# Attention and expert kernel: each unit in four stages a turn apart, state decay and kp on GpSimd, routing in four batches

## The chip, the cores and the metric

One core of one Trainium2 chip. The metric is device time in microseconds (us), from the first to the last instruction of the core. The engines are PE (TensorE matmuls; PEld its weight loads), DVE (VectorE), ACT (ScalarE), POOL (GpSimd) and SP (SyncE, whose queue issues most DMA transfers).

A run is called slow, and left out of the ratios, when it is over 1.5% above the fastest run of its kernel in the set; the others are called fast. Between sets on different chips the same kernel differed by up to 3%: the medians of the kernel before in the sets below are 473 to 488 us. So every comparison is made with runs of the kernel before on the same chip in the same set.

## The reference

A linear attention with a complex, data-dependent decay, then a mixture of experts that sends each row to its best expert. Batch 4, heads 8, sequence 768, head dimension 48; 8 experts of width 1024.

```python
mag = np.sqrt(a_re * a_re + a_im * a_im)
scale = np.minimum(mag, 0.999) / (mag + 1e-06)
a_re_n, a_im_n = a_re * scale, a_im * scale
for t in range(S):                                  # state S_re + i S_im, D x D for each head
    new_re = ar * S_re - ai * S_im
    new_im = ar * S_im + ai * S_re
    S_re, S_im = new_re + outer(k[t], v[t]), new_im
    y[t] = q[t] @ S_re
# rows of y -> logits by w_gate -> one expert for each row
out[row] = gate * relu(x[row] @ w1[e]) @ w2[e]
```

## The kernel before

The sequence is cut into 6 chunks of 128 steps, which with the 4 batches gives 24 units (g, b). Two units make a group: the elementwise work (logarithms, angles, exponentials) is done by group, and ScalarE loads its function tables twice for each. A unit then takes cumulative moduli and angles, and makes the scaled `Qh`, `KW` (whose first part is k scaled by `kp`), `V`:

```python
def hats(x, i):
    ...
    nc.vector.tensor_tensor(P[:], cs[:, i], both(pm[:, 0, i]), Alu.mult)        # 768 elements a partition
    nc.vector.tensor_tensor(kp[:], qk[:, 1, i], pm[:, 1, i], Alu.mult)          # 384
    ...
    nc.vector.tensor_tensor(Qh[:], P[:], both(qk[:, 0, i]), Alu.mult)
    nc.vector.tensor_tensor(KW[:, :, 0:C]..., cs[:, i], both(kp[:]), Alu.mult)
```

`front` transposes both on PE, copies them out on ScalarE and makes the masked product W at once; `back` makes Y and the new state, and the rows from Y at once:

```python
def front(g, b):                                    # transposes -> KT, QT -> W
    ...
            nc.scalar.copy(T[name][:, h4:h4 + 4], tp)
    ...
        nc.vector.tensor_tensor(KW[:, h4:h4 + 4, C:], wp, mask..., Alu.mult)

def back(g, b, KW, V, cB, QT):                      # Zs, Y and U, state, rows
    ...
            nc.scalar.copy(yT[:, js], py[:, :, C:])
    ...
        nc.vector.tensor_tensor(t1[:], U[:], cB[:, :, 0:1, :]..., Alu.mult)     # 384
        nc.vector.tensor_tensor(t2[:], U[:], cB[:, :, 1:2, :]..., Alu.mult)     # 384
        nc.vector.tensor_tensor(new[:, :, 0], t1[:, :, 0], t2[:, :, 1], Alu.add)       # 192
        nc.vector.tensor_tensor(new[:, :, 1], t1[:, :, 1], t2[:, :, 0], Alu.subtract)  # 192
    ...
        nc.tensor.matmul(xw[:, j, :], yT[:, j, :], sel[:, j, :], start=True, stop=True)
```

The text of the kernel gives the instructions and their dependencies. The order in which each engine issues them is chosen when the program is built, by a scheduler that places whatever it reckons to be ready first. The engines then keep to that order: in the trace of the changed kernel the loop's operations on VectorE (260), ScalarE (340) and GpSimd (140) all start in the built order.

Of the kernel before, what the change touches and what calls it, by code (L numbers as in the profile page):

```python
# [23 lines left out]
def gate_loop(nc, ctx, tc, cpool, ident, q, k, v, a_re, a_im, sel, lg, x_rows, casts, make_router):  # L24
# [120 lines left out]
    def moduli(x):  # L145
        cs, lm = box.pop(("cs", x))
        pm = el.tile([L, 2, NG, H, D], F32, name="pm")
# [10 lines left out]
    def hats(x, i):  # L158
# [7 lines left out]
        nc.vector.tensor_tensor(kp[:], qk[:, 1, i], pm[:, 1, i], Alu.mult)  # L166
# [3 lines left out]
        KW = un.tile([L, H, C + L], F32, name="KW", bufs=4)  # L170
        nc.vector.tensor_tensor(KW[:, :, 0:C].rearrange("t h (c d) -> t h c d", c=2), cs[:, i], both(kp[:]), Alu.mult)
        V = un.tile([L, H, 64], F32, name="V", bufs=4)
# [3 lines left out]
        if g < G - 1:  # L176
            cB = un.tile([128, J, 2, D], F32, name="cB", bufs=4)
            for u in range(2):
                nc.sync.dma_start(out=cB[u * 64:(u + 1) * 64].rearrange("p j c d -> p j (c d)"), in_=c_scr[g * B + b].rearrange("(j u c) -> u j c", u=2, c=C)[u][None].broadcast_to([64, J, C]))
        box["unit", g, b] = Qh, KW, V, cB  # L180

    def front(g, b):
        Qh, KW, V, cB = box.pop(("unit", g, b))
        T = {}
        for name, src in (("KT", KW[:, :, 0:C]), ("QT", Qh.rearrange("t h c d -> t h (c d)"))):
            T[name] = un.tile([C, H, L], F32, name=name)
            for h4 in range(0, H, 4):
# [3 lines left out]
                nc.scalar.copy(T[name][:, h4:h4 + 4], tp)  # L191
        for h4 in range(0, H, 4):
            wp = bank([L, 4, L], "wp")
            for i in range(4):
                for u in range(2):
                    nc.tensor.matmul(wp[u * 64:(u + 1) * 64, i, :], T["KT"][:, h4 + i, u * 64:(u + 1) * 64], T["QT"][:, h4 + i, :], start=True, stop=True)  # L196
            nc.vector.tensor_tensor(KW[:, h4:h4 + 4, C:], wp, mask[:, None, :].broadcast_to([L, 4, L]), Alu.mult)  # L197
        return KW, V, cB, T["QT"]
# [3 lines left out]
    def back(g, b, KW, V, cB, QT):  # L202
# [27 lines left out]
        if more:  # L230
            t1 = un.tile([128, J, 2, D], F32, name="t1", bufs=1)
            t2 = un.tile([128, J, 2, D], F32, name="t2", bufs=1)
            new = un.tile([128, J, 2, D], F32, name=f"state{b}", bufs=2)
            nc.vector.tensor_tensor(t1[:], U[:], cB[:, :, 0:1, :].broadcast_to([128, J, 2, D]), Alu.mult)
            nc.vector.tensor_tensor(t2[:], U[:], cB[:, :, 1:2, :].broadcast_to([128, J, 2, D]), Alu.mult)
            nc.vector.tensor_tensor(new[:, :, 0], t1[:, :, 0], t2[:, :, 1], Alu.add)
            nc.vector.tensor_tensor(new[:, :, 1], t1[:, :, 1], t2[:, :, 0], Alu.subtract)
            state[b] = new

        xw = bank([L, J, sel.shape[2]], "xw")  # L240
# [8 lines left out]
    NX = len(groups)  # L249
    EXP, TRIG = "natural_log_exp_and_others", "trig_and_small"  # L250
    table(EXP)
# [4 lines left out]
    table(TRIG)  # L256
    angles(0)
    rt = make_router(ctx, ps, bank)
    table(EXP)
    moduli(0)  # L260
    logs(1)
    load_a(2)
    for i in range(NG):
        hats(0, i)
    load_qk(1)
    table(TRIG)
    angles(1)
    made = front(*groups[0][0])
    open_ = []
    late = []  # L270
    w = 0
    for x in range(NX):
        for i, (g, b) in enumerate(groups[x]):
            w += 1
            ahead = front(*order[w]) if w < len(order) and i + 1 < NG else None
            if i == 0:

                table(EXP)
                if x + 1 < NX:
                    moduli(x + 1)  # L280
                for f in late:
                    f(act)
                late = []
                if x + 2 < NX:
                    logs(x + 2)
                    load_qk(x + 2)
                if x + 3 < NX:
                    load_a(x + 3)
            back(g, b, *made)
            if x + 1 < NX:  # L290
                hats(x + 1, i)
            if i == NG - 1:
                if x + 2 < NX:
                    table(TRIG)
                    angles(x + 2)
# [408 lines left out]
```

## Time and profile before

| | us |
|---|---|
| median of the runs, before | 473.3 (472.5 to 478.4) |
| profiled run | 476.2, clock 0.914 (a run marked slow) |
| last matmul of the rows ends | 343.7 |
| experts after it | 132.5 |
| a group in the loop, 158 to 315 us | 26.1 |

The loop over the units is the part that the change touches. The lines of the profile that carry this are in the prediction.

### The profile page before, as it was taken

What the parts mean: (1) busy time and instruction counts of PE and PEld (TensorE: products, weight loads), DVE (VectorE), ACT (ScalarE), POOL (GpSimd) and SP (SyncE); (2) the same over time, 40 slices, a digit from 0 to 9 for tenths busy, and PEclk for the clock granted to TensorE, in tenths of its full rate; (3) what the DMA queues carried; (4) which work ended last, traced back from release to release, by engine and by line L of the source; (5) the groups of instructions that cost most, each with busy time, mean ns of one, the idle gap of its engine ahead of it and who ended that gap; (6) DMA issues with size and microseconds to landing.
All of it is one profiled execution on the core that took longest, in us unless ns stands there. A gap on an engine that the chain in (4) does not pass through costs nothing.

```text
span 476.2 us, 8571 instructions
## 1 busy us (share of the span) xinstructions
PE 355.6 (75%) x3141; PEld 267.6 (56%) x3141; DVE 294.5 (62%) x673; ACT 259.6 (55%) x442; POOL 110.2 (23%) x138
## 2 busy tenths in 40 slices
PE   0518887678749698877978696989824998899874
PEld 0206564556636476655757484768613766667552
DVE  2683876869478887978797887765261433344321
ACT  3575767567736757776686758675312222223221
POOL 6401030200202002110202000000013566566512
PEclk9957889799979989998999899899955999999988
DMA  9979299987968899997999550100038799899991
GB/s 153 148 135 130 61 185 156 175 125 129 169 119 155 130 182 170 181 166 130 164 164 193 93 109 18 35 1 18 10 126 331 263 357 353 300 347 315 351 379 65
DMA packets 166844, 80.84 MB, mean 170 GB/s; under 512 B 145431, under 2 KB 157196, under 8 KB 166802
## 3 DMA queue, kind: packets, MB, share of 16 engines
q1 hardware_dynamic: 151810, 59.92, 53.3%
q0 software_dynamic: 14992, 20.37, 21.8%
q8 instruction: 25, 0.41, 0.4%
q14 instruction: 17, 0.14, 0.1%
HBM read 85.68 MB, written 21.12 MB: 224 GB/s over the span
## 4 chain that ended last, share of the span: by engine, by line
PE 32%; ACT 20%; issue 16%; DVE 15%; DMA 8%; POOL 6%; SPq 2%; POOLq 0%; DVEq 0%; ACTq 0%
PE wp L196 7%; PE py L218 5%; ACT sq L82 5%; PE xw L242 5%; ACT KT L191 4%; DMA xg<-x_rows,idx 3%; PE u L136 3%; POOL xg L573 3%; POOL out_dram L615 3%; DMA ab<-in_a_im_dram 3%; DVE s L111 2%; PE py L221 2%; DVE Qh L169 2%; ACT L79 2%; PE tKT L190 2%
## 5 line engine op out<-in xcount | busy, mean ns | idle before, releaser
L218 PE MATMUL py<-KW,V 128*64 128x224 f32 x384 | 63.6, 390 | 0.0
L196 PE MATMUL wp<-QT,KT 96*64 96x128 f32 x768 | 48.7, 281 | 14.6 <-ACT QT L191 14.1
L197 DVE TENSOR_TENSOR KW<-wp,mask 128x512 f32<-128x512 f32 x48 | 32.9, 688 | 37.6 <-PE wp L196 37.4
L196 PEld LDWEIGHTS wp<-QT,KT 96*64 96x64 f32 x768 | 42.5, 139 | 20.8 <-ACT QT L191 20.8
L242 PE MATMUL xw<-sel,yT 128*128 128x104 f32 x192 | 34.4, 309 | 25.7 <-ACT yT L229 25.6
L596 PE MATMUL h_ps<-xgT,w1t 128*128 128x256 bf16 (+1 forms) x456 | 47.7, 266 | 4.3 <-DMA w1t<-w1b 4.3
L242 PEld LDWEIGHTS xw<-sel,yT 128*128 128x128 f32 x192 | 27.9, 206 | 38.8 <-ACT yT L229 31.8
L136 PE MATMUL u<-tan,turn 128*128 128x384 f32 x48 | 25.3, 615 | 31.7 <-ACT tan L82 31.7
L221 PE MATMUL py<-QT,Zs 96*48 96x128 f32 x320 | 37.7, 283 | 13.4 <-ACT Zs L208 13.3
L596 PEld LDWEIGHTS <-w1t 128*128 128x128 bf16 x456 | 40.1, 103 | 11.5 <-DMA w1t<-w1b 5.5
L600 ACT ACTIVATE hT<-h_ps 128x512 bf16<-128x512 f32 x31 | 18.5, 597 | 50.2 <-PE h_ps L596 44.3
L607 PE MATMUL y_ps<-w2t,hT 128*128 128x384 bf16 x248 | 43.7, 327 | 2.3 <-DMA w2t<-w2b 2.3
L573 POOL DMA_INDIRECT xg<-x_rows,idx x31 | 30.1, 972 | 60.5 <-ACT idx L559 51.3
L191 ACT COPY KT<-tKT 96x512 f32<-96x512 f32 x48 | 25.8, 581 | 32.7 <-PE tKT L190 32.6
L615 POOL DMA_INDIRECT out_dram<-y_sb,idx x31 | 31.4, 1013 | 47.0 <-ACT y_sb L611 42.7
L598 DVE TENSOR_SCALAR hT<-h_ps 128x512 bf16<-128x512 f32 x31 | 21.4, 692 | 29.2 <-PE h_ps L596 28.1
L218 PEld LDWEIGHTS py<-KW,V 128*64 128x64 f32 x384 | 32.9, 148 | 10.4 <-issue 4.7
L115 POOL TENSOR_SCALAR neg<-ab 128x768 bf16<-128x768 f32 x12 | 25.7, 2143 | 54.5 <-DMA ab<-in_a_re_dram 32.2
L221 PEld LDWEIGHTS py<-QT,Zs 96*48 96x48 f32 x320 | 25.0, 128 | 22.4 <-ACT Zs L208 17.6
L173 POOL MEMSET V<- 128x128 f32 x24 | 4.7, 203 | 135.3 <-PE py L218 89.4
L79 ACT ACT_TABLE_LOAD x27 | 34.6, 1283 | 1.3 <-PEq L688 0.8
L607 PEld LDWEIGHTS <-hT 128*128 128x128 bf16 x248 | 23.5, 98 | 17.0 <-issue 1.5
(135 smaller groups left out, 700.4 us busy)
## 6 DMA issues: line engine op xcount, KB each, us to landing
w1t<-w1b SPq DMA_DIRECT2D x19, 768.0 KB
w2t<-w2b SPq DMA_DIRECT2D x19, 768.0 KB
w1b<-in_moe_w_dram POOLq DMA_DIRECT2D x8, 768.0 KB, 7.9
w2b<-in_moe_w_dram POOLq DMA_DIRECT2D x8, 768.0 KB, 9.3
ab<-in_a_re_dram SPq DMA_DIRECT2D x24, 192.0 KB
ab<-in_a_im_dram SPq DMA_DIRECT2D x24, 192.0 KB
qk<-in_q_dram SPq DMA_DIRECT2D x24, 192.0 KB
qk<-in_k_dram SPq DMA_DIRECT2D x24, 192.0 KB
```

The lines of the kernel that those rows point to most:

```text
L79: then(nc.scalar.preload_act_table_set(name))
L136: nc.tensor.matmul(u, turn[:], tan[:, i], start=True, stop=False)
L191: nc.scalar.copy(T[name][:, h4:h4 + 4], tp)
L196: nc.tensor.matmul(wp[u * 64:(u + 1) * 64, i, :], T["KT"][:, h4 + i, u * 64:(u + 1) * 64], T["QT"][:, h4 + i, :], start=True, stop=True)
L197: nc.vector.tensor_tensor(KW[:, h4:h4 + 4, C:], wp, mask[:, None, :].broadcast_to([L, 4, L]), Alu.mult)
L218: nc.tensor.matmul(py[u * 64:(u + 1) * 64, i, :], V[:, 2 * j + u, :], KW[:, 2 * j + u, :], start=True, stop=(g == 0))
L221: nc.tensor.matmul(py[u * 64:u * 64 + D, i, C:], Zs[:, j, u * 64:u * 64 + D], QT[:, 2 * j + u, :], start=False, stop=True)
L242: nc.tensor.matmul(xw[:, j, :], yT[:, j, :], sel[:, j, :], start=True, stop=True)
L573: nc.gpsimd.indirect_dma_start(out=xg[:], out_offset=None, in_=x_rows, in_offset=bass.IndirectOffsetOnAxis(ap=idx[:, s, 0:1], axis=0))
L596: nc.tensor.matmul(h_ps[:, f, :], w1t[:, k, ff * 128:(ff + 1) * 128], xgT[:, k, :], start=(k == 0), stop=(k == KD - 1))
L607: nc.tensor.matmul(y_ps[:], hT[:, f, s * 128:(s + 1) * 128], w2t[:, f, :], start=(f == 0), stop=(f == NF - 1))
L615: sc = nc.gpsimd.indirect_dma_start(out=out, out_offset=bass.IndirectOffsetOnAxis(ap=idx[:, s, 1:2], axis=0), in_=y_sb[:], in_offset=None, ...
```

## The change

The intent: spread a unit over more turns, so that no engine waits for what another has just begun (W finds its transposes, the rows find Y, both made a turn earlier); relieve VectorE by moving `kp` and the state decay to GpSimd, which is mostly idle; and fewer, larger routing batches. Buffers are shifted to make room. The core of the diff:

```diff
-        nc.vector.tensor_tensor(kp[:], qk[:, 1, i], pm[:, 1, i], Alu.mult)
+        nc.gpsimd.tensor_tensor(kp[:], qk[:, 1, i], pm[:, 1, i], Alu.mult)
 ...
-    def front(g, b):
+    def values(g, b):      # V, cB                 (buffers 4 -> 3)
+    def turned(g, b):      # transposes, KT, QT
+    def inner(g, b):       # W
 ...
-    def back(g, b, KW, V, cB, QT):
+    def outer(g, b):       # Zs, Y, U, state
 ...
-            nc.vector.tensor_tensor(t1[:], U[:], cB..., Alu.mult)
-            nc.vector.tensor_tensor(t2[:], U[:], cB..., Alu.mult)
-            nc.vector.tensor_tensor(new[:, :, 0], t1[:, :, 0], t2[:, :, 1], Alu.add)
-            nc.vector.tensor_tensor(new[:, :, 1], t1[:, :, 1], t2[:, :, 0], Alu.subtract)
+            nc.gpsimd.tensor_tensor(t1[:], U[:], cB..., Alu.mult)
+            nc.gpsimd.tensor_tensor(t2[:], U[:], cB..., Alu.mult)
+            nc.gpsimd.tensor_tensor(new[:, :, 0], t1[:, :, 0], t2[:, :, 1], Alu.add)
+            nc.gpsimd.tensor_tensor(new[:, :, 1], t1[:, :, 1], t2[:, :, 0], Alu.subtract)
+    def rows(g, b):        # rows, logits
 ...
+    takes = {7: 0, 15: 8, 19: 16, 23: 20}          # routing batches of 8, 8, 4 and 4 tiles, not six of 4
+    for w in range(NU + 1):
+        unit(values, w + 1)
+        unit(turned, w + 2)
+        unit(inner, w + 1)
+        unit(outer, w)
+        unit(rows, w - 1)
+        if w % NG == 0:
+            exps(w // NG + 2)
+        hat(w + 3)
+        if w % NG == NG - 1:
+            trigs(w // NG + 3)
```

More of the change, by code (lines that the diff above doesn't have):

```diff
@@ L146, in moduli @@
         cs, lm = box.pop(("cs", x))
-        pm = el.tile([L, 2, NG, H, D], F32, name="pm")
+        pm = el.tile([L, 2, NG, H, D], F32, name="pm", bufs=1)
         for i in range(NG):
@@ L169, in hats @@
         nc.vector.tensor_tensor(Qh[:], P[:], both(qk[:, 0, i]), Alu.mult)
-        KW = un.tile([L, H, C + L], F32, name="KW", bufs=4)
+        KW = un.tile([L, H, C + L], F32, name="KW", bufs=5)
         nc.vector.tensor_tensor(KW[:, :, 0:C].rearrange("t h (c d) -> t h c d", c=2), cs[:, i], both(kp[:]), Alu.mult)
-        V = un.tile([L, H, 64], F32, name="V", bufs=4)
+        box["hats", g, b] = Qh, KW
+    def values(g, b):
+        V = un.tile([L, H, 64], F32, name="V", bufs=3)
         nc.gpsimd.memset(V[:, :, D:64], 0.0)
@@ L176, in hats @@
         if g < G - 1:
-            cB = un.tile([128, J, 2, D], F32, name="cB", bufs=4)
+            cB = un.tile([128, J, 2, D], F32, name="cB", bufs=3)
             for u in range(2):
                 nc.sync.dma_start(out=cB[u * 64:(u + 1) * 64].rearrange("p j c d -> p j (c d)"), in_=c_scr[g * B + b].rearrange("(j u c) -> u j c", u=2, c=C)[u][None].broadcast_to([64, J, C]))
-        box["unit", g, b] = Qh, KW, V, cB
-    def front(g, b):
-        Qh, KW, V, cB = box.pop(("unit", g, b))
+        box["values", g, b] = V, cB
+    def turned(g, b):
+        Qh, KW = box.pop(("hats", g, b))
         T = {}
-        for name, src in (("KT", KW[:, :, 0:C]), ("QT", Qh.rearrange("t h c d -> t h (c d)"))):
-            T[name] = un.tile([C, H, L], F32, name=name)
+        for name, src, bufs in (("KT", KW[:, :, 0:C], 2), ("QT", Qh.rearrange("t h c d -> t h (c d)"), 3)):
+            T[name] = un.tile([C, H, L], F32, name=name, bufs=bufs)
             for h4 in range(0, H, 4):
@@ L191, in front @@
                 nc.scalar.copy(T[name][:, h4:h4 + 4], tp)
+        box["turned", g, b] = KW, T["KT"], T["QT"]
+    def inner(g, b):
+        KW, KT, QT = box.pop(("turned", g, b))
         for h4 in range(0, H, 4):
@@ L195, in front @@
                 for u in range(2):
-                    nc.tensor.matmul(wp[u * 64:(u + 1) * 64, i, :], T["KT"][:, h4 + i, u * 64:(u + 1) * 64], T["QT"][:, h4 + i, :], start=True, stop=True)
+                    nc.tensor.matmul(wp[u * 64:(u + 1) * 64, i, :], KT[:, h4 + i, u * 64:(u + 1) * 64], QT[:, h4 + i, :], start=True, stop=True)
             nc.vector.tensor_tensor(KW[:, h4:h4 + 4, C:], wp, mask[:, None, :].broadcast_to([L, 4, L]), Alu.mult)
-        return KW, V, cB, T["QT"]
+        box["inner", g, b] = KW, QT
     state = {}
-    def back(g, b, KW, V, cB, QT):
+    def outer(g, b):
+        KW, QT = box.pop(("inner", g, b))
+        V, cB = box.pop(("values", g, b))
         if g:
@@ L232, in back @@
             t2 = un.tile([128, J, 2, D], F32, name="t2", bufs=1)
-            new = un.tile([128, J, 2, D], F32, name=f"state{b}", bufs=2)
-            nc.vector.tensor_tensor(t1[:], U[:], cB[:, :, 0:1, :].broadcast_to([128, J, 2, D]), Alu.mult)
-            nc.vector.tensor_tensor(t2[:], U[:], cB[:, :, 1:2, :].broadcast_to([128, J, 2, D]), Alu.mult)
-            nc.vector.tensor_tensor(new[:, :, 0], t1[:, :, 0], t2[:, :, 1], Alu.add)
-            nc.vector.tensor_tensor(new[:, :, 1], t1[:, :, 1], t2[:, :, 0], Alu.subtract)
+            new = un.tile([128, J, 2, D], F32, name=f"state{b}", bufs=1)
+            nc.gpsimd.tensor_tensor(t1[:], U[:], cB[:, :, 0:1, :].broadcast_to([128, J, 2, D]), Alu.mult)
+            nc.gpsimd.tensor_tensor(t2[:], U[:], cB[:, :, 1:2, :].broadcast_to([128, J, 2, D]), Alu.mult)
+            nc.gpsimd.tensor_tensor(new[:, :, 0], t1[:, :, 0], t2[:, :, 1], Alu.add)
+            nc.gpsimd.tensor_tensor(new[:, :, 1], t1[:, :, 1], t2[:, :, 0], Alu.subtract)
             state[b] = new
+        box["outer", g, b] = yT
+    def rows(g, b):
+        yT = box.pop(("outer", g, b))
         xw = bank([L, J, sel.shape[2]], "xw")
@@ L249, in gate_loop, with exps, trigs, unit @@
     NX = len(groups)
+    NU = len(order)
     EXP, TRIG = "natural_log_exp_and_others", "trig_and_small"
+    open_ = []
+    late = []
+    takes = {7: 0, 15: 8, 19: 16, 23: 20}
+    def exps(x):
+        if x < NX + 1:
+            table(EXP)
+        if x < NX:
+            moduli(x)
+        for f in late:
+            f(act)
+        late.clear()
+        if x + 1 < NX:
+            logs(x + 1)
+            load_qk(x + 1)
+        if x + 2 < NX:
+            load_a(x + 2)
+    def trigs(x):
+        if x < NX:
+            table(TRIG)
+            angles(x)
+    def unit(stage, w):
+        if 0 <= w < NU:
+            stage(*order[w])
+    def hat(w):
+        if w < NU:
+            hats(w // NG, w % NG)
     table(EXP)
@@ L255, in gate_loop @@
     load_qk(0)
-    table(TRIG)
-    angles(0)
-    rt = make_router(ctx, ps, bank)
-    table(EXP)
-    moduli(0)
-    logs(1)
-    load_a(2)
-    for i in range(NG):
-        hats(0, i)
-    load_qk(1)
-    table(TRIG)
-    angles(1)
-    made = front(*groups[0][0])
-    open_ = []
-    late = []
-    w = 0
-    for x in range(NX):
-        for i, (g, b) in enumerate(groups[x]):
-            w += 1
-            ahead = front(*order[w]) if w < len(order) and i + 1 < NG else None
-            if i == 0:
-                table(EXP)
-                if x + 1 < NX:
-                    moduli(x + 1)
-                for f in late:
-                    f(act)
-                late = []
-                if x + 2 < NX:
-                    logs(x + 2)
-                    load_qk(x + 2)
-                if x + 3 < NX:
-                    load_a(x + 3)
-            back(g, b, *made)
-            if x + 1 < NX:
-                hats(x + 1, i)
-            if i == NG - 1:
-                if x + 2 < NX:
-                    table(TRIG)
-                    angles(x + 2)
-                if w < len(order):
-                    ahead = front(*order[w])
-            made = ahead
-            for _ in range(1):
-                if casts:
-                    cast = casts.pop(0)()
-                    tc.add_manual_dep(cast.ins, chain[-1].ins.name, mybir.DependencyInfo(mybir.DependencyClass.Sync, mybir.DependencyReason.DATA), reason="spreads the casts over the turns")
-            open_ = [t for t in open_ if next(t, True) is None]
-            if b == B - 1:
-                open_.append(rt.take(g * B, (g + 1) * B, late))
-                next(open_[-1])
@@ L307, in gate_loop @@
-    table(EXP)
+    trigs(0)
+    exps(0)
+    hat(0)
+    hat(1)
+    unit(turned, 0)
+    trigs(1)
+    rt = make_router(ctx, ps, bank)
+    exps(1)
+    hat(2)
+    unit(inner, 0)
+    unit(turned, 1)
+    trigs(2)
+    unit(values, 0)
+    for w in range(NU + 1):
[9 more added lines that the diff above has]
+            trigs(w // NG + 3)
+        if casts:
+            cast = casts.pop(0)()
+            tc.add_manual_dep(cast.ins, chain[-1].ins.name, mybir.DependencyInfo(mybir.DependencyClass.Sync, mybir.DependencyReason.DATA), reason="spreads the casts over the turns")
+        open_ = [t for t in open_ if next(t, True) is None]
+        if w - 1 in takes:
+            open_.append(rt.take(takes[w - 1], w, late))
+            next(open_[-1])
@@ L346, in __init__ @@
         rc = self.rc = ctx.enter_context(tc.tile_pool(name="rc", bufs=1))
-        self.rp = ctx.enter_context(tc.tile_pool(name="rp", bufs=3))
+        self.rp = ctx.enter_context(tc.tile_pool(name="rp", bufs=2))
         self.tile_of = [b * G + g for g in range(G) for b in range(B)]
@@ L395, in take @@
         last = m1 == len(self.tile_of)
-        M = 4
+        M = 8
         def t(name, shape, dt=F32):
@@ L420, in take @@
             so_far.append(self.acc)
-            acc = rp.tile([TP, E], BF16, name="acc", bufs=16)
+            acc = rp.tile([TP, E], BF16, name="acc", bufs=20)
             if self.acc is None:
@@ L462, in take @@
         for i in range(n):
-            lo = rp.tile([TP, 2, 128], BF16, name="lo", bufs=4)
+            lo = rp.tile([TP, 2, 128], BF16, name="lo", bufs=8)
             nc.vector.tensor_scalar(lo[:, 0], self.iob[:, 0:128], part[:, 0, i:i + 1], self.p1[:], Alu.is_equal, Alu.mult)
             nc.vector.tensor_scalar(lo[:, 1], self.iob[:, 0:128], part[:, 0, i:i + 1], float(TP * self.tile_of[m0 + i]), Alu.is_equal, Alu.mult)
-            hi = rp.tile([TP, self.NC], BF16, name="hi", bufs=4)
+            hi = rp.tile([TP, self.NC], BF16, name="hi", bufs=8)
             nc.vector.tensor_scalar(hi[:], self.iob[:, 0:self.NC], part[:, 1, i:i + 1], None, Alu.is_equal)
```

## The prediction

> **What bounds the kernel now.** I read the page's busy line and slices first, to see where each engine and the DMA are full.
>
> ```profile
> PE 355.6 (75%) x3141; PEld 267.6 (56%) x3141; DVE 294.5 (62%) x673; ACT 259.6 (55%) x442; POOL 110.2 (23%) x138
> ...
> PE   0518887678749698877978696989824998899874
> ...
> DVE  2683876869478887978797887765261433344321
> ACT  3575767567736757776686758675312222223221
> POOL 6401030200202002110202000000013566566512
> ...
> DMA  9979299987968899997999550100038799899991
> ```
>
> A slice is 11.9 us. Slices 0 to 3 are the start-up, 4 to 28 the attention loop, the rest the experts. In the loop no engine is full; the DMA row is nearly full up to slice 21, and almost empty after. The change touches only the first 344 us.
>
> Then the busy time of each engine by stretch (columns: stretch, length, PE, PEld, DVE, ACT, POOL busy, clock, DMA share, GB/s):
>
> ```profile
> 158.00:210.00 52.00, 42.36 (x414) 33.22 (x410) 43.39 (x102) 37.32 (x62) 8.21 (x10) 0.97 0.99 165
> 210.00:262.00 52.00, 42.37 (x409) 32.90 (x406) 43.15 (x103) 37.07 (x61) 8.22 (x10) 0.97 0.93 162
> 262.00:315.00 53.00, 43.50 (x405) 33.78 (x405) 41.02 (x100) 37.07 (x61) 0.82 (x4) 0.94 0.30 57
> ```
>
> Each stretch is two groups of two units. Per group: DVE 21.6 us, PE 21.2, ACT 18.6, DMA 24.2 to 25.7. Now the chain of waits, for the pace: the modulus matmul (ls) opens each group.
>
> ```profile
> 124.50 8.56 DMA ab<-in_a_im_dram
> ...
> 158.47 0.86 PE ls L150 x2
> ...
> 210.17 0.86 PE ls L150 x2
> ...
> 261.81 0.86 PE ls L150 x2
> ...
> 314.90 0.86 PE ls L150 x2
> ...
> 342.48 1.18 PE xw L242 x8
> ```
>
> From 158.47 to 314.90 six groups pass: 26.1 us a group, with the DMA full (two stretches) and with it at 0.30 (the third). So DMA does not set this pace; a relay between PE, ACT and DVE does, and DMA adds a stall now and then (8.56 us at 124.50). The relay shows in the page's idle column:
>
> ```profile
> L197 DVE TENSOR_TENSOR KW<-wp,mask 128x512 f32<-128x512 f32 x48 | 32.9, 688 | 37.6 <-PE wp L196 37.4
> L242 PE MATMUL xw<-sel,yT 128*128 128x104 f32 x192 | 34.4, 309 | 25.7 <-ACT yT L229 25.6
> L221 PE MATMUL py<-QT,Zs 96*48 96x128 f32 x320 | 37.7, 283 | 13.4 <-ACT Zs L208 13.3
> L196 PE MATMUL wp<-QT,KT 96*64 96x128 f32 x768 | 48.7, 281 | 14.6 <-ACT QT L191 14.1
> ```
>
> W waits for the copies of the transposes made just before it, the rows waited 25.6 us for yT made just before them, Y for Zs. These are what the stages a turn apart should remove.
>
> **What the Trainium skill says.** "GPSIMD Engine Reference", section 3.1: a tensor_tensor add of 2048 fp32 takes 4497 ns on GpSimd against 2293 ns on VectorE, about twice. The trace before has no two-input work on GpSimd; its one large op, neg (768 elements), takes 2.13 us. "SBUF — State Buffer", section "Who interferes with whom": a VectorE instruction with two SBUF inputs contends with a GpSimd instruction that reads SBUF, and the later one blocks until the first is done. The trace agrees only in part: under a neg of 2.21 us, tan took 1.57 us instead of 0.96, and a one-hot 0.60 instead of 0.19, so some 0.4 to 0.6 us lost, not the whole. "DMA: Bandwidth & Descriptors", Specifications: full rate needs transfers of at least 512 B. Here 145431 of 166844 packets are under that: the first 50 us moved 38071 packets of about 180 bytes with the DMA 90% busy, so 1.18 ns each over 16 engines, at 135 GB/s; the experts' large ones run above 300.
>
> **The change part by part.**
>
> DVE. Per group it loses two kp (0.551 us), four state products (0.552) and four state sums (0.352): 1.10 + 2.21 + 1.41 = 4.7 us. It goes from 21.6 to 16.9 us.
>
> GpSimd. It gains them. An estimate from the skill's 2.2 ns an element, with a little dispatch: 0.95 us for 384 elements, 0.55 for 192, so 6 x 0.95 + 4 x 0.55 = 7.9 us. With neg 2.1, two memsets 0.4 and two cast issues 0.71 and 0.86, about 12 us of a group: half busy, not a bound. Its reads (10 us) meet some 10 us of DVE's two-input work; at random 10 x 10 / 25 = 4 us of overlap, half of it paid by DVE: 19 us, still under the pace. The state is needed four turns later, so its slower decay is hidden; kp is behind P and Qh (1.9 us) on DVE and mostly hidden.
>
> PE. Its work is the same. The instruction order of the changed kernel is now: transposes of unit w+2, W of w+1, state transposes, half of Y of w, rows of w-1, rest of Y. W finds KT and QT, and the rows find yT, made a turn earlier. In throughput a turn is 1.8 (16 transposes) + 2.0 (W) + 0.6 + 2.8 (state and Y) + 1.25 (rows) = 8.4 us, plus 3.4 a group for u and ls: 20.2 us a group. What remains is one serial piece a group: rows, table load 1.28, tan 0.85, u 2.3, fr 1.1, cs 1.8, table 1.28, exps.
>
> ACT. 18.6 us of work a group is unchanged. Walking its new order from the end of tan: it must wait 3.3 us until u and the first transposes have passed PE; about 1 us for the second ls, behind Y; and about 1 us in small waits for U and for s. 18.6 + 5.3 = 24 us a group.
>
> DMA. The same packets. With casts, 24.2 to 25.7 us a group, and the 16 casts still sit in the first 16 turns. So those eight groups can hardly go below 25; the ninth, without casts, takes ACT's 24.
>
> Start-up. The new prologue does one more group of elementwise work before the loop. In the trace before, the table for the exps of group 1 ends at 43.7 us, 19.9 us after that of group 0 (23.8). One more such round is 63.6, and the first U and yT copies (1.5 us) give 65 for the exps of group 2; before, they come at 76.
>
> End. In the changed kernel the exps of group 11, the last, come at turn 18, with PE already some way into the turn: 2.7 us of it left, then three full turns without elementwise work at 8.7, then 6.8, 4.8 and 1.3 us as the stages run out: 41.7 us. Before, 343.7 - 315.8 = 28 us remain there.
>
> Sum: 65 + 9 x 25.0 + 41.7 = 331.7 us at the last row matmul, against 343.7 (342.48 + 1.18) before: 12 us less. Routing in four batches of 4 or 8 in place of six of 4 saves two sets of about 14 small DVE operations of 0.17 us (5 us) off the path; the last batch is still four tiles, so the 132 us after it do not move. 473.3 - 12 = **461 us**.
>
> **The rivals.**
>
> One: DMA becomes the bound. For it: 0.99 and 0.93 busy at the present pace, and the 8.56 us wait for ab. If each cast group takes 25.7 us and stalls come on top (26.4), the sum is 344: no gain, about 473. Against it: in 50 to 262 us the share is 0.91, so about 19 us are idle, and casts may fall behind into the turns after 16, where DMA is nearly free. If they do, ACT's 24 us hold throughout: 65 + 216 + 41.7 = 323, or 452 us.
>
> Two: GpSimd in order becomes a relay. neg waits for DMA (32.2 us in total before), casts wait for ACT, and kp, the V memset (so V's load, now issued only a turn ahead with three buffers instead of four) and the state stand behind them. One late ab load then delays kp, KW and the transposes. With the port lock slower than my estimate this costs 1 to 2 us a group: 27 us a group, 65 + 243 + 41.7 = 350, or 479 us.
>
> Three: DVE was the true bound, and 4.7 us less is worth nearly all of it: 26.1 - 4.7 = 21.4 us a group, 65 + 193 + 41.7 = 300, or 430. Against it: DMA cannot serve that in the cast groups, and PE needs 20.2 with a serial piece besides.
>
> **Range and chances.** The pace of a group decides: 24 gives 452, 25 gives 461, 26 gives 470; the start-up may be off by 3 us and the end by 4. Range 449 to 473. Faster by over 2% is under 463.9, that is a pace under 25.3: 0.60. Within 2% (up to 482.8): 0.33. Slower: 0.07.
>
> **What would show it.** Right: the ls marks 24 to 25 us apart, ACT the best filled engine with its idle time at the transposes' copies after tan, DMA at 0.95 or more up to about 255 us, the waits of W on QT and of the rows on yT nearly gone, DVE near 19 us and GpSimd near 12 us a group, exps of group 2 near 65 us, last rows near 332. Wrong: marks at 26 with DMA full (rival one); DVE's two-input operations clearly longer than 0.95 us, or PE waiting for transposes' inputs through kp (rival two); marks at 22 or less, which would say that DMA's busy share is not a service limit; or the last 132 us moving at all.

## The result, and the profile after

The changed kernel takes 494.3 us (493.8 to 497.3, four fast runs) against 472.9 of the kernel before in the same set. The ratio is 1.048, with a 95% interval of 1.042 to 1.054: slower by 4.8%. A ratio here is always the mean time of one kernel's fast runs over the mean of the other's fast runs of the same rounds, so it is not quite the ratio of the medians. The profiled run after is fast (492.6 us); that of before, a slow one, would make the loss look smaller than it is.

The page after, the busy line and the slices of GpSimd and the DMA engines:

```profile
PE 359.8 (73%) x3141; PEld 269.0 (55%) x3141; DVE 284.2 (58%) x539; ACT 259.2 (53%) x439; POOL 223.9 (45%) x242
...
POOL 6243063744646446454364636262004176566612
...
DMA  9949646979697797849949785112007699999992
```

The same work, and a POOL row that is now half full in the loop; but the DMA row, which was nearly full before up to slice 21, has gaps. The same stretches as in the prediction (columns: stretch, length, PE, PEld, DVE, ACT, POOL busy, clock, DMA share, GB/s):

```profile
158.00:210.00 52.00, 41.21 (x349) 30.25 (x349) 36.66 (x81) 32.95 (x52) 24.45 (x27) 0.84 0.85 146
210.00:262.00 52.00, 37.45 (x299) 27.41 (x298) 33.50 (x53) 29.85 (x49) 25.70 (x25) 0.81 0.71 120
262.00:315.00 53.00, 43.56 (x415) 33.29 (x414) 39.22 (x66) 37.56 (x61) 27.38 (x28) 0.93 0.72 124
```

In the first two stretches every engine but POOL does less than before, and DMA is at 0.71 to 0.85: they wait for each other. The pace can be read from ScalarE's timeline, where a table load opens the exponentials of each group; this is the one of group 2 and the one of group 11:

```profile
64.68 1.28 ACT L79 ACT_TABLE_LOAD   x1
...
318.21 1.28 ACT L79 ACT_TABLE_LOAD   x1
```

Nine groups in 253.5 us: **28.2 us a group**. I call this the pace below. The last matmuls of the rows, those of two units, start at 360.33 and end at 362.4; the experts take 130.2 us after them.

The groups of instructions that answer to those of the prediction (columns after the bars: busy us, mean ns of one; idle time just before them and what ended it):

```profile
L203 PE MATMUL wp<-QT,KT 96*64 96x128 f32 x768 | 47.2, 276 | 0.0
L230 PE MATMUL py<-QT,Zs 96*48 96x128 f32 x320 | 35.9, 307 | 24.4 <-ACT Zs L217 24.4
L204 DVE TENSOR_TENSOR KW<-wp,mask 128x512 f32<-128x512 f32 x48 | 32.1, 683 | 11.8 <-PE wp L203 11.8
L255 PE MATMUL xw<-sel,yT 128*128 128x104 f32 x192 | 28.7, 291 | 0.0
L171 DVE TENSOR_TENSOR KW<-cs,kp 128x768 f32<-128x768 f32 x24 | 28.3, 1178 | 19.2 <-POOL kp L166 19.2
```

The stages did what they were made for: the rows waited 25.7 us for `yT` before and wait for nothing now, W on PE waited 14.6 us and waits for nothing, the mask on VectorE went from 37.6 us to 11.8. One wait that they were to remove has nearly doubled: Y on PE waited 13.4 us for `Zs` before and waits 24.4 now. New are 19.2 us in which VectorE waits for `kp` from GpSimd, and `KW` itself has grown from a mean of 945 ns to 1178. One such wait, in VectorE's timeline, with what stood behind it:

```profile
235.86 0.96 DVE L164 TENSOR_TENSOR P<-cs,pm 128x768 f32<-128x768 f32 x1 [1.06 <-ACT pm L82]
...
245.43 0.96 DVE L171 TENSOR_TENSOR KW<-cs,kp 128x768 f32<-128x768 f32 x1 [7.21 <-POOL kp L166]
246.30 1.75 DVE L113 TENSOR_TENSOR tan<-ab 128x768 f32<-128x768 f32 x1
247.97 1.74 DVE L164 TENSOR_TENSOR P<-cs,pm 128x768 f32<-128x768 f32 x1
249.64 1.74 DVE L111 TENSOR_TENSOR s<-sq 128x768 f32<-128x768 f32 x1
```

and in the same moment on GpSimd:

```profile
242.30 2.13 POOL L115 TENSOR_SCALAR neg<-ab 128x768 bf16<-128x768 f32 x1 [9.18 <-DMA ab<-in_a_re_dram]
244.41 0.98 POOL L166 TENSOR_TENSOR kp<-qk,pm 128x384 f32<-128x384 f32 x1
...
245.51 1.73 POOL L243 TENSOR_TENSOR t<-U,cB 128x384 f32<-128x384 f32 x1
247.20 1.70 POOL L244 TENSOR_TENSOR t<-U,cB 128x384 f32<-128x384 f32 x1
```

GpSimd waits with `neg` for a transfer, `kp` behind it comes late, `KW` on VectorE waits 7.21 us, and `s` behind that comes late; ScalarE, which needs `s`, then idles 9.09 us. After that both engines run their two-input operations in alternation: 1.7 us each instead of 0.95 and 1.0. So this view shows two suspects at once, a wait for GpSimd and the contention of the two engines. Which of them the 3 us a group are, or whether it is something else that the view doesn't show, needed experiments.

### The profile page after: what moved, and what is told of

Read it like the earlier page. It is cut to its first block, busy times and chain, and to the rows that moved or that the text cites. A ratio compares the mean times of both kernels' runs of the same rounds, so it can differ in the third digit from the quotient of the medians.

```text
span 492.6 us, 8581 instructions
## 1 busy us (share of the span) xinstructions
PE 359.8 (73%) x3141; PEld 269.0 (55%) x3141; DVE 284.2 (58%) x539; ACT 259.2 (53%) x439; POOL 223.9 (45%) x242
## 4 chain that ended last, share of the span: by engine, by line
PE 30%; issue 18%; DVE 15%; ACT 11%; POOL 10%; DMA 7%; SPq 7%; POOLq 0%; DVEq 0%; ACTq 0%
PE py L227 4%; PE u L136 4%; PE wp L203 4%; DMA xg<-x_rows,idx 3%; PE py L230 3%; PE xw L255 3%; PE tKT L193 3%; POOL out_dram L641 3%; DVE Qh L169 3%; DVE s L111 3%; POOL xg L599 2%; ACT sq L82 2%; PE y_ps L633 2%; PE tQT L193 2%; DVE P L164 2%
## 5 line engine op out<-in xcount | busy, mean ns | idle before, releaser
L136 PE MATMUL u<-tan,turn 128*128 128x384 f32 x48 | 33.8, 802 | 65.2 <-ACT tan L82 65.2
L227 PE MATMUL py<-KW,V 128*64 128x224 f32 x384 | 55.1, 377 | 0.0
L115 POOL TENSOR_SCALAR neg<-ab 128x768 bf16<-128x768 f32 x12 | 28.7, 2393 | 55.8 <-PE tQT L193 14.4
L230 PE MATMUL py<-QT,Zs 96*48 96x128 f32 x320 | 35.9, 307 | 24.4 <-ACT Zs L217 24.4
L136 PEld LDWEIGHTS u<-tan,turn 128*128 128x128 f32 x48 | 12.4, 290 | 73.3 <-ACT tan L82 52.2
L166 POOL TENSOR_TENSOR kp<-qk,pm 128x384 f32<-128x384 f32 x24 | 29.0, 1213 | 32.7 <-ACT pm L82 32.7
L230 PEld LDWEIGHTS py<-QT,Zs 96*48 96x48 f32 x320 | 22.8, 137 | 37.4 <-ACT Zs L217 26.9
L171 DVE TENSOR_TENSOR KW<-cs,kp 128x768 f32<-128x768 f32 x24 | 28.3, 1178 | 19.2 <-POOL kp L166 19.2
L204 DVE TENSOR_TENSOR KW<-wp,mask 128x512 f32<-128x512 f32 x48 | 32.1, 683 | 11.8 <-PE wp L203 11.8
L82 ACT ACTIVATE sq<-sq 128x768 f32<-128x768 f32 x24 | 20.2, 843 | 31.2 <-DVE s L111 31.2
L193 PE MATMUL tKT<-ident,KW 128*96 128x128 f32 x192 | 30.9, 315 | 6.8 <-DVE KW L171 6.8
L193 PEld LDWEIGHTS tKT<-ident,KW 128*96 128x96 f32 x192 | 26.4, 149 | 15.4 <-DVE KW L171 7.4
```

The lines of the kernel that those rows point to most:

```text
L82: then(nc.scalar.activation(*args, **kw))
L136: nc.tensor.matmul(u, turn[:], tan[:, i], start=True, stop=False)
L166: nc.gpsimd.tensor_tensor(kp[:], qk[:, 1, i], pm[:, 1, i], Alu.mult)
L193: nc.tensor.transpose(tp[:, i, :], src[:, h4 + i], ident[:])
L204: nc.vector.tensor_tensor(KW[:, h4:h4 + 4, C:], wp, mask[:, None, :].broadcast_to([L, 4, L]), Alu.mult)
L227: nc.tensor.matmul(py[u * 64:(u + 1) * 64, i, :], V[:, 2 * j + u, :], KW[:, 2 * j + u, :], start=True, stop=(g == 0))
```

## The experiments

The theory that I began with: the stages gain, and GpSimd takes the gain back, by the contention and by its place in order. The rival: the stages themselves, or their smaller buffers, cost time. Eighteen kernels were run, because the cause changed twice on the way. "E1" and so on below are their numbers. Each was run in three rounds and gave the right result. The experts' stretch at the end is left out of the argument: it was 130 to 144 us long, by the chip of the set more than by the kernel, and the kernel before was slower on the same chips.

### E1 to E4: which part costs?

E1 is the changed kernel with `kp` and the state decay back on VectorE; stages, buffers and batches stay.

```diff
-        nc.gpsimd.tensor_tensor(kp[:], ...)          # and the four of the state decay
+        nc.vector.tensor_tensor(kp[:], ...)
```

> The changed kernel with kp and the state decay back on VectorE; stages, buffers and routing batches stay. Theory A (the work on GpSimd costs: it holds the SBUF port against VectorE and stands in order before kp): the pace of a group falls from 28.1 us to 25 or 26 and the time to 465 to 476 us. Rival B (the stages, the smaller buffers or the queue orders cost): 488 to 496 us.

Measured: 457.1 us against 481.6, ratio **0.947** (0.938 to 0.955), pace 23.3 us (62.70 to 272.69 over nine groups). That is below the range that I gave to my own theory, too. The rival is out: the stages gain 5%. Two stretches of it:

```profile
105.00:158.00 53.00, 47.67 (x448) 36.20 (x446) 40.45 (x74) 41.60 (x67) 10.12 (x12) 0.94 1.01 174
...
210.00:262.00 52.00, 44.10 (x455) 33.83 (x452) 45.29 (x93) 42.15 (x71) 6.06 (x9) 1.00 1.01 176
```

PE is busy 47.7 of 53 us and 44.1 of 52, where it was 39 to 44 in such stretches before and 37 to 44 after.

E2 puts only the state decay back on VectorE, so `kp` is on GpSimd; E3 only `kp`, so the state is on GpSimd.

> The changed kernel with only the state decay back on VectorE; kp stays on GpSimd. Theory A with the state as the main part (85 us of GpSimd's busy time, against 29 of kp): 470 to 480 us. If kp's place on the path is the main part: 485 to 492. Rival B: 488 to 496.

> The changed kernel with only kp back on VectorE; the state decay stays on GpSimd. Theory A with the state as the main part: 483 to 492 us. If kp's relay is the main part: 468 to 478. Rival B: 488 to 496.

Measured: E2 1.009 (0.996 to 1.023), pace 26.2; E3 0.996 (0.984 to 1.009), its profile from a slow run. Against E1 `kp` costs about 6% and the state about 5%, and together about 10% (1.048 to 0.947). Each alone eats the stages' whole gain.

E4 moves `kp` and the state to GpSimd in the kernel before, with nothing else of the change.

> The kernel before with kp and the state decay moved to GpSimd, nothing else. Theory A: slower than before, by 10 to 25 us (483 to 498). Rival B: VectorE loses 4.7 us a group of its work and nothing is paid for it, 455 to 473 us.

Measured: 1.078 (1.066 to 1.090), 524.6 us in the median, far above what I expected. The move costs 8% without the stages, where it costs 10 points with them.

### E5, E6, E9: the contention alone

If GpSimd's work hurts by contending with VectorE for SBUF, idle work that nobody waits for hurts as well. E5 is E1 with four idle GpSimd operations a unit of the state's sizes, started when the unit's last `yT` copy is done; E6 the same with three memsets of about the same length, which read nothing; E9 one idle multiply of `kp`'s size, started when the second exponential of the unit is done.

```diff
+            first = nc.gpsimd.tensor_tensor(idle[:, 0], src[:, 0:384], src[:, 0:384], Alu.mult)   # E5: two of 384, two of 192
+            first = nc.gpsimd.memset(idle[:], 0.0)                                               # E6: three of 960
+        first = nc.gpsimd.tensor_tensor(idle[:], src[:, 0:384], src[:, 0:384], Alu.mult)          # E9: one of 384
```

> The stages with everything on VectorE (0.9468 of before), plus idle work on GpSimd that nobody reads: in each unit two products of 384 and two sums of 192 elements from SBUF, released by the copy of yT, where the state decay would be. Port theory (a GpSimd instruction that reads SBUF and a two-input VectorE instruction shut each other out): ratio to before 0.98 to 1.01, as with the real state decay there (0.9963), and VectorE's P, Qh and KW at 1.07 us or more in the mean. Queue theory (the state's late results, its cB buffers and the order of the queues cost, not the port): 0.945 to 0.96.

> The same with idle work that only writes: three memsets of 960 elements per unit in the same place, about 3 us of GpSimd time. Port theory for reads: no loss, 0.94 to 0.955, and P, Qh and KW at 0.95 us. If GpSimd being busy in order ahead of neg and the V memset is what costs: 0.97 to 1.0.

> All routines on VectorE in the four stages (the first experiment, 0.947 of the kernel before, a group every 23.3 us), plus one GpSimd multiply of 384 elements per unit that reads a constant tile, starts when the second exponential of the unit is done (as the real kp would), and that nobody waits for. The real kp on GpSimd cost the four stages about 6% (0.947 to 1.009). If that was the shared SBUF port (the multiply makes the concurrent VectorE operations slower), this idle one costs most of it too: a ratio of 0.985 to 1.01, P, Qh and KW at 1.05 us or more against 0.95. If it was the relay (VectorE's KW waits in order for a GpSimd result), the ratio stays at 0.945 to 0.96 and the group within 0.5 us of 23.3. I expect a split nearer the relay: 0.96 to 0.975, a group every 24 us.

Measured: E5 0.971 (0.963 to 0.980), pace 24.9; E6 0.943 (0.938 to 0.948), pace 23.3; E9 0.966 (0.959 to 0.974), pace 24.1. The group of `Qh` in E5, then in E6:

```profile
L169 DVE TENSOR_TENSOR Qh<-P,qk 128x768 f32<-128x768 f32 x24 | 26.1, 1088 | 0.0
```

```profile
L169 DVE TENSOR_TENSOR Qh<-P,qk 128x768 f32<-128x768 f32 x24 | 22.8, 951 | 0.0
```

With reads beside it, `Qh` takes 1088 ns; with writes alone beside it, 951, the same as in E1 (952). So the contention is real, is one of reads, and costs about 2.5 points for the state's size and 2 for `kp`'s. But the real state costs 5% and the real `kp` 6%. Over half is still to find.

A check that proved important later: the built programs of E5, E6 and E9 have exactly E1's order of instructions on VectorE, ScalarE and PE. Idle work changes no order.

### E7, E8, E10: buffers

E7 is E3 (state on GpSimd) with four buffers of `cB` in place of three. E8 is the changed kernel with four of `V` and `cB`, as before the change. E10 is E7 with two each of `U`, `t1` and `t2`.

```diff
-            cB = un.tile([128, J, 2, D], F32, name="cB", bufs=3)      # E7, E8 (there V too), E10
+            cB = un.tile([128, J, 2, D], F32, name="cB", bufs=4)
-            U = un.tile([128, J, 2, D], F32, name="U", bufs=1)        # E10; t1, t2 too
+            U = un.tile([128, J, 2, D], F32, name="U", bufs=2)
```

> Stages with the state decay on GpSimd and kp on VectorE (0.9963), now with four cB buffers in place of three, so that the cB load need not wait on the queue for the state decay (34.1 us of waits there). Port theory: 0.98 to 1.0, little changed. Queue theory: 0.95 to 0.97.

> The changed kernel with four V and four cB buffers, as before, and the rest as it is. If the smaller buffers cost: 0.99 to 1.02 in place of 1.048. Port theory: 1.03 to 1.05.

> State decay on GpSimd, kp on VectorE, four buffers of cB as in the seventh experiment (0.988, a group every 25.8 us), and now two buffers each of U, t1 and t2 in place of one, so that VectorE's next update of U need not wait until GpSimd has read the last. If single buffers were the part of the state's cost that the idle reads did not show (0.988 against 0.971), the ratio falls to 0.97 to 0.975. If the cost is the port alone, because the real operations lie beside the sums that ScalarE waits for, it stays at 0.98 to 0.995. I expect the second.

Measured: E7 0.988 (0.981 to 0.995), pace 25.8; E8 1.050 (1.041 to 1.059); E10 0.989 (0.981 to 0.996), pace 25.7. More buffers give the changed kernel nothing, and the state at most one per cent. Buffers are not it.

### E11, E12: batches and transfers

E11 is E1 with six routing batches of four tiles, as before.

```diff
-    takes = {7: 0, 15: 8, 19: 16, 23: 20}
+    takes = {3: 0, 7: 4, 11: 8, 15: 12, 19: 16, 23: 20}
```

> The first experiment with the routing in six batches of four tiles, as before the change, in place of four batches. One batch is about 20 small VectorE operations plus work for each tile, so two batches more are some 40 operations of 0.1 to 0.2 us with their waits, 5 to 8 us of VectorE over the loop. If the batching was a part of the gain: 0.955 to 0.965. If VectorE has slack for it where the DMA queue is the bound: 0.942 to 0.952, the same as the first experiment. I expect the second.

Measured: 0.952 (0.947 to 0.957), pace 23.7 where E1 has 23.3. The batches are worth half a per cent at most, within the intervals.

E12 is E1 with the casts of the expert weights started in the ninth turn, not the first, to see whether the full DMA engines set E1's pace.

```diff
-        if casts:
+        if casts and w >= 8:
```

> The first experiment with the sixteen casts of the weights started one a turn from the ninth turn on, not from the first. In the first experiment the DMA engines are full (shares of 0.97 to 1.06) from 74 to 260 us and nearly empty (0.13) from 260 to 335. If the DMA engines bound its pace of 23.3 us, the groups of the first eight turns now come every 20 to 22 us and the work of the last casts falls into the empty stretch: 0.91 to 0.935. If ScalarE or VectorE bound it (19 to 20 us of 23.3 busy each) with their waits on each other, the pace stays at 22.5 to 23.3: 0.94 to 0.95. If the weights come too late for the experts, the last stretch, 131 us in every kernel so far, grows. I expect 0.925.

Measured: 0.935 (0.928 to 0.942); the profile is of a slow run, with a pace of 23.2. One early stretch:

```profile
105.00:158.00 53.00, 47.70 (x452) 35.36 (x450) 41.41 (x79) 41.46 (x68) 6.22 (x7) 0.94 0.52 101
```

The DMA share falls from 1.01 to 0.52 in this stretch and PE's work in it stays at 47.7 us. A full DMA did not bound E1. The ratio's gain over E1 is within what the intervals allow, and I draw nothing from it. My expectation also said that the experts' stretch was 131 us in all kernels; in the profiles of that set (E9 to E12) it was 138 to 144.

### E13 to E15: is it the wait behind neg?

The stall shown above has `kp` behind `neg`, which waits for a transfer. E13 is E2 (`kp` on GpSimd) with `neg` on VectorE, E15 is E1 with the same (the control), E14 the changed kernel with the same.

```diff
-        nc.gpsimd.tensor_scalar(neg[:], ab[:, 0], 0.0, None, Alu.is_lt)
+        nc.vector.tensor_scalar(neg[:], ab[:, 0], 0.0, None, Alu.is_lt)
```

> The second experiment (four stages, kp on GpSimd, state decay on VectorE: 1.009, a group every 26.2 us) with the comparison neg moved from GpSimd to VectorE. In the second experiment neg stood waiting on GpSimd for the transfer of ab for up to 14.4 us with kp behind it, and KW on VectorE once waited 8.5 us for kp. If that order is what kp costs beyond the port, the ratio falls by most of the 4%, to 0.965 to 0.985, and a group takes 24 to 25 us. If kp costs by something else (its own latency, the port), it stays at 1.00 to 1.015. I expect 0.98.

> The control: the first experiment (nothing of the change on GpSimd, 0.947, 23.3 us) with neg on VectorE too. neg is 12 operations of 768 elements, at most 0.95 us each on VectorE by its other operations of that size, against 2.1 us on GpSimd. VectorE had 3 to 4 us free in a group: 0.94 to 0.955, no change. A fall below 0.935 would mean that neg's time on GpSimd was itself on the path, and the run before must then be read against this one.

> The changed kernel as it is (1.048, 28.2 us) with neg alone moved to VectorE. If neg before kp in GpSimd's order is the relay, some 3 to 4% come back: 1.00 to 1.02. The port's 4.5% and the rest of the state's stay, so that it doesn't come down to 0.97. If the order is not the cause: 1.04 to 1.055. I expect 1.015.

Measured: E13 0.997 (0.989 to 1.005), pace 26.0; E15 0.948 (0.939 to 0.957), pace 23.4 to E1's 23.3; E14 1.039 (1.029 to 1.048), pace 28.2. The most visible stall of the trace is worth about one per cent, where I expected 3 to 4. In E13, `KW` waits for `kp` just 1.8 us in all, and the kernel still runs 5% slower than E15. My theory of a late GpSimd result fell here.

### E16 to E18: the order of issue

E13 has another thing in which it differs from E15, which no view of the profile names: its order. I compared the built programs. The dependencies are the same, one instruction a unit is on another engine, but the scheduler has placed much else differently: on VectorE 313 pairs of instructions stand the other way round in E2 as against E1 (counting pairs within 80 places), in E3 415, in the changed kernel 426; on the SP queue 129, 169 and 191; on ScalarE some 90, and on PE, which has far more instructions, 270, 202 and 100. (E15's order differs from E1's as well, in 101 pairs on VectorE, at the same pace: not any other order costs time.) And with idle work, none on VectorE, ScalarE and PE. So every kernel with real work moved to GpSimd differs in two things, where the work is and in what order all the rest is issued.

These three pin the order of one kernel on another, on VectorE, ScalarE, PE and the SP queue, by dependencies that set the order alone and make nothing wait for completion. The built programs were compared: all instructions that both have stand in the same order.

```diff
+    for names in ISSUED.values():             # the order of the other kernel, engine by engine
+        prev = None
+        for n in names:
+            i = traced.get(f"I-{n}")
+            ...
+                tc.add_manual_dep(i, prev.name, ...NoSync..., reason="order of another kernel")
+            prev = i
```

E16 is E2 (`kp` on GpSimd) with E1's order. E17 is E1 (all on VectorE) with E2's order. E18 is the changed kernel with E1's order.

> The second experiment (kp on GpSimd, 1.009, a group every 26.2 us) with the issue order on VectorE, ScalarE, TensorE and the DMA queue pinned to that of the first experiment (0.947, 23.3 us), so that only the engine of kp differs from it. If the other issue order was what kp cost beyond the port, this comes to the 0.966 of the idle reads, 0.96 to 0.975, a group every 24 to 24.5 us. If it is the wait of KW for GpSimd (latency, order on GpSimd), the pinned order makes that wait worse, as KW now stands sooner after kp: 1.00 to 1.03. I expect 0.985, between them.

> The counterpart: the first experiment (kp and state on VectorE, 0.947) with the issue order of the second pinned on it, so that nothing is moved to GpSimd and only the order is another. If the order is what costs: 0.975 to 0.995. If the order is harmless: 0.94 to 0.955. I expect 0.965.

> The changed kernel as it is (1.048, 28.2 us), with kp and the state decay on GpSimd and the issue order of the first experiment pinned on VectorE, ScalarE, TensorE and the DMA queue. By the idle reads the port costs 2% and 2.5%: if the order is the rest, 0.99 to 1.01. If waits for GpSimd are: 1.04 or more. I expect 1.02.

Measured, with those that they are set against (ratio to the kernel before, pace):

| placement | E1's order | the order that the scheduler chose when the work was moved |
|---|---|---|
| all on VectorE | E1: 0.947, 23.3 us | E17, with E2's order: 0.991, 25.1 us |
| kp on GpSimd | E16: 0.968, 23.9 us | E2: 1.009, 26.2 us |
| kp and state on GpSimd | E18: **0.975**, 24.6 us | the changed kernel: **1.048**, 28.2 us |

The intervals of the three new ones are 0.953 to 0.983 (E16), 0.977 to 1.005 (E17) and 0.960 to 0.990 (E18), wider than the others: four of the seven runs of the kernel before in that set were slow (488 to 492 us), and the ratios rest on the other three (476 to 482). The paces say the same without them. All three kernels came out further on the side of the order than I expected (0.985, 0.965, 1.02). Read along the first line: the order alone, with not one instruction moved to another engine, costs 4.4 points. Read down the first column: with a good order, `kp` on GpSimd costs 2 points, as much as the idle multiply of E9 costs (0.966), so the dependency on GpSimd costs nothing that these runs can tell from the contention; and `kp` and state together cost 2.8. Of the 10 points between E1 and the changed kernel, 7 are order.

How an order costs time can be seen in E17, which has nothing new on GpSimd. VectorE's waits over its nine groups (columns: us in total, times, longest; in these three kernels the lines are shifted, L316 and L317 are `tan`, L375 `KW`, L370 `kp`, L315 `s`):

```profile
DVE tan L316 <- DMA ab<-in_a_im_dram: 9.5, 4, 4.4
DVE tan L316 <- DMA V<-in_v_dram: 8.1, 2, 4.2
```

In E1 the one such wait is this:

```profile
DVE tan L113 <- DMA ab<-in_a_im_dram: 3.3, 1, 3.3
```

VectorE stops at `tan` for transfers 17.6 us in place of 3.3. Those 14.3 us more are nearly the 15.7 us by which E17's nine groups are longer (1.74 us each). The sizes fit; that these waits are the loss is argued, as VectorE is not full and no run removes them alone. The changed kernel, and E18 with the same work on GpSimd in E1's order, by VectorE's wait for `kp` and ScalarE's for `s` over their nine groups; first the changed kernel:

```profile
DVE KW L171 <- POOL kp L166: 16.0, 5, 7.2
```
```profile
ACT KT L194 <- PE tKT L193: 36.0, 13, 4.5
ACT sq L82 <- DVE s L111: 28.1, 9, 9.1
ACT yT L238 <- DVE U L235: 12.4, 10, 4.1
```

and E18:

```profile
DVE KW L375 <- POOL kp L370: 2.0, 3, 1.5
```
```profile
ACT KT L398 <- PE tKT L397: 35.9, 13, 5.0
ACT yT L442 <- DVE U L439: 7.6, 11, 1.3
...
ACT sq L286 <- DVE s L315: 2.4, 2, 2.1
```

With the order pinned ScalarE waits 26 us less for `s`; the nine groups are 32 us shorter (28.17 less 24.61, nine times). The wait of Y for `Zs`, 24.4 us in the changed kernel, is 4.4 in E18. The built programs show what stands before `s`: on VectorE, in each of the last seven groups of the changed kernel, one more `P` and one more `KW` (once two) are placed ahead of it than in E1's order, and `KW` is what waits for `kp`. The stall at 245 us shown above is one such case; that all nine waits for `s` are of this kind was not shown.

At the same time the contention did not become less, rather more: `KW` in E18 takes

```profile
L375 DVE TENSOR_TENSOR KW<-cs,kp 128x768 f32<-128x768 f32 x24 | 32.0, 1335 | 2.0 <-POOL kp L370 2.0
```

1335 ns to 1178 in the changed kernel, and E18 is 7 points faster.

What stays open: which engine's order it is. VectorE's and the SP queue's differ most, and an order chosen for one engine moves the others when the program is built. No kernel that pins one engine alone was run.

GpSimd's own queue was not pinned: 33 pairs of its instructions stand the other way round in E18 as against the changed kernel, so its order is a part of what E18 changes. A control for the pins, E1 with E1's order, was not run; E16 and E18 carry the same pins, and they got faster. The granted clock of PE is a rival that was not tested: over the nine groups it was 0.93 in E1 and 0.90 in E17, 0.91 in E18 and 0.86 in the changed kernel, and PE's busy time was 180.5, 185.7, 185.8 and 194.7 us. By these figures, at most some 5 of E17's 15.7 us, and 9 of the 32 us between the changed kernel and E18, are PE taking longer for the same work; whether the clock made the groups longer, or the waits made the clock lower, no run separates.

The line of the table for the changed kernel's own order with all work on VectorE was not run either, so that order and placement simply add up is shown for `kp` only. And the state's cost beyond contention in E7 and E10 (0.988 to E5's 0.971) was not retried in E1's order; that it is order too is only likely.

The fastest kernels here are E1 and its variants E6, E12 and E15, at 0.935 to 0.948 of the kernel before: the stages, with nothing moved to GpSimd. They don't differ among each other by more than their intervals.

## Why the prediction was wrong, point by point

Predicted: 461 us, 449 to 473. Measured: 494. By its own sum, 65 + 9 x 25.0 + 41.7:

- **Start, 65 us: right within the 3 us given.** The table load of group 2 is at 64.7, its exponentials, which the 65 means, at 66.9.
- **End, 41.7 us: right.** From the table load of group 11 at 318.2 to the end of the last rows at 362.4 it is 44.2; from its exponentials at 321.1, 41.3.
- **The last 132 us unmoved: right.** 130.2.
- **Nine groups at 25.0 us: wrong.** 28.2, so 28.5 us too few between the table loads; that, with 0.3 less at the start and 2.5 more at the end, is the whole difference from 331.7 to 362.4 at the last row matmul.

Inside the pace, by the steps that led to it:

- **VectorE from 21.6 to 16.9 us of work a group, 19 with the contention: right.** It is busy 180.7 us of the 265 from 50 to 315 us, which is 19.2 a group of 28.2. GpSimd is busy 13.9 us a group, where I said about 12. The contention inside this is larger than the 2 us that I gave: an estimate from the means of the same operations here and in E1 is 2.9 us a group of longer VectorE operations. What the idle work of E5 and E9 costs the pace is 1.55 and 0.7 us.
- **The failed step: the walk along ScalarE, 18.6 us of work and 5.3 of waits, "24 us a group", and in it the term "about 1 us in small waits for U and for s".** ScalarE's work was right, 18.4 us a group. Its waits are 9.5: 4.0 for the transposes (3.3 predicted), 0.5 for the second `ls` (1), 0.4 for the rows' logits (not in the sum), and 4.5 for `s` and `U`, of which 3.1 for `s`. That term was mis-sized by 3.5 us a group. The prediction gives PE's order and walks ScalarE's; that VectorE would come through P, Qh, then KW, with `kp` "behind P and Qh (1.9 us) on DVE and mostly hidden", and give `s` in time, I took from the text of the kernel, not from VectorE's built order. In that order a further `KW`, which waits for `kp`, stands ahead of `s` in the last seven groups, and ScalarE waits 28 us for `s`. In E18, with the same work on the same engines in E1's order, the same term is 1.1 us, and the pace 24.6: the walk's number fits an order that the changed kernel did not have. That E18 comes so near it is in part luck, as its other terms are off by up to 0.7 us, some up and some down.
- **DMA, "can hardly go below 25": wrong, though it did no harm here.** E1 runs at 23.3 with a share of 1.01, and no faster with 0.52.
- **The first rival (DMA the bound): out.** Shares of 0.71 to 0.85.
- **The second rival (GpSimd in order becomes a relay, 27 us a group, 479 us): the nearest, and still the wrong mechanism.** Its stall stands in the trace, `neg` before `kp`; taking `neg` away gave back 0.9 points in the changed kernel, within the intervals. The wait of `KW` for `kp` that it named is real, but E1's order takes it from 16.0 us to 2.0 with the same work on GpSimd. That I gave this rival too little chance followed from the same walk.
- **The third rival (VectorE the bound): out.** With all its work back on it, the kernel is the fastest.

## What to carry to other kernels

Where a scheduler chooses the order of issue, moving one operation to another engine is two changes: compare the built order of all engines before blaming the engine that got the work, and pin the old order to tell the two apart. The longest stall in a trace can be a symptom: take it away before believing in it. And a move to an idle engine has to be worth its contention: idle work with the same reads, tied to the same moment and waited for by nobody, measures that without changing the order.

## What the Trainium skill lacked or had wrong

- "SBUF — State Buffer", section "Who interferes with whom", agrees where both operations have two inputs: a VectorE operation with two SBUF inputs contends with a GpSimd operation that reads SBUF, and one blocks the other. In the changed kernel both alternate at 1.7 us each, 0.95 and 1.0 alone. Beside `neg`, which reads one input, it does not always hold: in the kernel before, `tan` from two SBUF inputs at 236.01 us took 0.96 us wholly inside a `neg` of 2.13 us (from 235.22), so that neither was longer, as far as the rough spans of GpSimd tell. That GpSimd work that only writes does not contend, as the page says, is confirmed by E6: 951 ns beside memsets, 952 without. What the page lacks is what it costs a pipelined kernel: with one two-input operation of 384 elements a unit about 2% (E9), with four of 1152 elements in all 2.5% (E5).
- "GPSIMD Engine Reference", section 3.1, has 4497 ns for an add of 2048, so 2.2 ns an element; 384 elements took 0.98 us and 192 took 0.59 at the shortest, 2.6 and 3.1 ns an element. The page has no `tensor_tensor` as small as these, and beside VectorE's work the means were 1.21 to 1.36 us (384).
- The same page, section 4.1, says that one-input work on GpSimd is "roughly line-rate". `neg`, one input of 768 fp32 elements written as bf16, took 2.13 us on GpSimd at the shortest, 2.8 ns an element where two-input `kp` took 2.6, and 0.57 us (mean) on VectorE in E15.
- No page that I read treats the order of issue that is chosen at build time as something that a change of engine alters: 4.4 points for `kp`'s order alone (E17), 7 for the whole change (E18).
